# Two output chunks leave PSUM through ScalarE, and the first group's down products stand in another order

## The chip, the cores and the metric

The kernel runs on one core of a Trainium2 chip. The metric is device time in microseconds (us) of one execution. The engines of a core work side by side, each through its own queue of instructions in order, and wait for each other through semaphores: TensorE (PE, matrix products into PSUM banks), VectorE (DVE), ScalarE (ACT), GpSimd (POOL) and SyncE (SP, whose queue here issues most DMA transfers). PEld is TensorE's loading of weights, which runs beside its products.

## The reference

A gated linear recurrence per batch and head, then a layer with a softmax-weighted activation, a norm and a second product:

```python
for t in range(S):                       # S = 768, B = 4, H = 8, D = 48
    state = alpha[:, :, t, :, None] * state + k[:, :, t] (outer) v[:, :, t]
    y[:, :, t] = q[:, :, t] @ state
x = y.transpose(0, 2, 1, 3).reshape(B * S, H * D)        # 3072 x 384
h = x @ w_in                                             # 3072 x 1024
solu = h * softmax(h)
ln = (solu - mean(solu)) / sqrt(var(solu) + 1e-6) * g_ln
out = ln @ w_out                                         # 3072 x 384
```

All in float32 on the device; the weights come as float64 and are turned into float32 by bit operations.

## The kernel before

**Tiling.** The 768 tokens are cut into G = 6 groups of 128 per batch; one group holds 4 batches x 128 = 512 tokens. A *chunk* n = 4g + b is the 128 tokens of batch b in group g. For each group the kernel does the attention part, then the `up` product (eight blocks f of 128 columns of h, each 128 x 512), and the `down` product per chunk: eight steps f accumulate 128 x 385 in one PSUM bank (`down`, L491; column 385 is the sum of the row that the norm needs). `down(n, half)` does four steps; with `part` only some of them. In float32 each step is two TensorE instructions.

**Attention of a group a.** `alpha_T` (L202, VectorE) transposes alpha; `scan_back` (L221, three scans on VectorE) makes the products of the decays; `keys_T` and `keys` (L234, L238, VectorE and GpSimd) make the scaled keys; `scan_on` (L225, three scans, i = 2, 0, 1) makes the factors of the queries, and with i = 2 also the small ScalarE copy `fend` (L231). `decay` (L253, GpSimd) scales the running state; `scores` (L272, TensorE) writes four PSUM banks `a0` to `a3`; `masked` (L286, VectorE) moves them to SBUF under the causal mask; `read_state` and `read_values` (L327, L340, TensorE) make y in the same four banks, and ScalarE copies y to `x` (L348), which `up` reads. `next_state` (L350) adds the group's keys and values to the state.

**Activation.** `up_act` (L392): ScalarE takes the exp e of h from PSUM (L400), VectorE u = h e (L401), ScalarE u squared (L402). `running` sums e and u squared; `token_sums` (L444) turns those sums into one number per token.

**`finish(n)`** (L502): VectorE copies the row sum out of the bank, forms the variance (three small operations, L514 to L519), and, in group 0 only, adds the mean correction into an SBUF tile `o_mean` (L523, reading the bank); GpSimd takes the power -1/2 (L527), ScalarE scales into `o_sb` (L529), SP writes it out (L530). There are two `o` banks (`ps_o`, two buffers), so `down` of chunk n + 2 can start only when chunk n has left its bank. Tiles named `o_mean` and `o_sb` have two buffers each.

**Checks.** The fast path is valid only where alpha lies in range and the float64 weights do. `alpha_over(g)` (L207, ScalarE, two passes over 128 x 1536) counts alphas outside; the next `load(alpha, an, g + 1)` overwrites what it reads, so that load (four DMAs on SP) waits for it. `in_range(i)` (L569, ScalarE, four instructions) does the like for the weight piece i. Nothing but the end of the kernel waits for their counts.

**What sets the order.** It is written out by hand: `tc.manual_schedule()` keeps each engine's instructions in program order. Group 0 and the attention of groups 1 and 2 are straight code (L639 to L804). `mean(0)` and `mean(1)` (L615) make the mean of the weights' rows; `tq` are the transposed queries. From group 1 on, a loop over g and eight steps s reads from a table which pieces of attention of group g + 1 go where (`first` for g = 1, L814; `usual` for the later ones, L808): `head` comes ahead of the step's `up`, `behind` after it, `middle` and `tail` around the step's `down`.

Of the kernel before, what the change touches and what calls it, by code (L numbers as in the profile page):

```python
# [9 lines left out]
FP = mybir.dt.float32  # L10
# [6 lines left out]
P = 128  # L17
# [15 lines left out]
def fast_path(ctx, tc, q, k, v, alpha, moe_w_in, moe_w_out, moe_g_ln, out):  # L33
# [12 lines left out]
    nc = tc.nc  # L46
    B, H, S, D = q.shape
    NTOK, DM = out.shape
# [8 lines left out]
    HF = FC // 2  # L57
# [4 lines left out]
    def pool(name, bufs, **kw):  # L62
        return ctx.enter_context(tc.tile_pool(name=name, bufs=bufs, **kw))
# [4 lines left out]
    work = pool("work", 2)  # L68
# [31 lines left out]
    an = const.tile([P, H, TQ, D], FP, name="an")  # L100
# [33 lines left out]
    st = [dict() for _ in range(N)]  # L134
# [3 lines left out]
    def load(src, dst, g):  # L138
        t = slice(g * P, (g + 1) * P)
        for b in range(B):  # L140
            nc.sync.dma_start(
                out=dst[32 * b : 32 * b + 32].rearrange("t h u d -> t h (u d)"),
                in_=src[b, :, t, :].rearrange("h (t u) d -> t h (u d)", u=TQ),
            )
# [62 lines left out]
    def alpha_over(g):  # L207
        x = an.rearrange("p h u d -> p (h u d)")
        sq = one.tile([P, 768], FP, name="sq").bitcast(U8)[:, 0 : x.shape[1]]
        for i, sign in enumerate((1.0, -1.0)):  # L210
            nc.scalar.activation(  # L211
                out=sq, in_=x, func=AF.Relu, scale=sign, bias=mone, accum_out=over[:, g, i : i + 1]
            )
# [12 lines left out]
    def scan_on(g, i):  # L226
        part = slice(NP * i, NP * i + NP)
        if i == 2:

            nc.vector.reciprocal(out=seed[:, :, 0:1], in_=h4[:, :, 1:2])  # L230
            nc.scalar.copy(out=fend[:, g], in_=h4[:, :, 1])  # L231
        scan(aT[:, part], aT[:, part], seed[:, part], False)
# [33 lines left out]
    def quarter(b):  # L266
        return slice(32 * b, 32 * b + 32)
# [4 lines left out]
    def scores(g, half, a=None):  # L272
        a = a or banks("a", [NP, P])
        for i in range(NP):
            h = half * NP + i
            for kb, qb in ((h, h), (H + h // 2, H + h)):
                for b in range(B):
                    nc.tensor.matmul(  # L278
                        a[b][:, i], lhsT=kT[quarter(b), kb], rhs=qv[quarter(b), qb], start=kb == h, stop=kb != h,
                        tile_position=(32 * b, 0), skip_group_check=True,  # L280
                    )
        masks[half] = a
# [11 lines left out]
    def keys_back(g, t=None):  # L294
        t = t or banks("tp", [NP, P], 3)
        for j in range(NB):
            nc.tensor.transpose(out=t[j // NP][:, j % NP], in_=kT[:, j], identity=ident)  # L297
        for i in range(3):
            nc.scalar.copy(out=kg[:, NP * i : NP * i + NP], in_=t[i])
# [191 lines left out]
    def down(n, half, part=slice(0, HF)):  # L491
        g, b = divmod(n, B)
        d = st[n]
        if half == 0 and part.start == 0:
            d["o"] = ps_o.tile([P, 512], FP, tag="o", name="o")
        for f in range(half * HF + part.start, half * HF + part.stop):
            nc.tensor.matmul(  # L497
                d["o"][:, 0 : DM + 1], lhsT=u_of(g, f)[:, b * P : b * P + P], rhs=w_out[:, f], start=(f == 0),
                stop=(f == FC - 1), skip_group_check=True,
            )  # L500

    def finish(n):  # L502
        g, b = divmod(n, B)
        d = st[n]
        s, o = sums[:, n], d["o"][:, 0:DM]
        t0 = b * S + g * P
        if g == G - 1:
            o_sb = work.tile([P, DM], FP, name="o_sb")
            r = gr[g]["r"][:, b : b + 1]
            nc.scalar.activation(out=o_sb, in_=o, func=AF.Copy, scale=r)  # L510
            nc.scalar.dma_start(out=out[t0 : t0 + P, :], in_=o_sb)
            d.clear()
            return
        nc.vector.tensor_copy(out=s[:, 0:1], in_=d["o"][:, DM : DM + 1])  # L514
        t = small.tile([P, 1], FP, name="t")
        nc.vector.scalar_tensor_tensor(
            out=t, in0=s[:, 0:1], scalar=-1.0 / DFF, in1=s[:, 0:1], op0=ALU.mult, op1=ALU.mult
        )
        nc.vector.tensor_tensor(out=s[:, 3:4], in0=t, in1=gr[g]["s"][:, b : b + 1], op=ALU.add)  # L519
        if g == 0:  # L520

            o = work.tile([P, DM], FP, name="o_mean")
            nc.vector.scalar_tensor_tensor(  # L523
                out=o, in0=mean_sb, scalar=s[:, 0:1], in1=d["o"][:, 0:DM], op0=ALU.mult, op1=ALU.add
            )
        r = small.tile([P, 1], FP, name="r")
        nc.gpsimd.tensor_tensor(out=r, in0=s[:, 3:4], in1=mhalf, op=ALU.pow)  # L527
        o_sb = work.tile([P, DM], FP, name="o_sb")
        nc.scalar.activation(out=o_sb, in_=o, func=AF.Copy, scale=r)  # L529
        nc.sync.dma_start(out=out[t0 : t0 + P, :], in_=o_sb)  # L530
        d.clear()
# [35 lines left out]
    made = {}  # L567

    def in_range(i):  # L569


        if not float64:
            return
        hi = raws[i][:, :, :, 1].bitcast(FP)
        sq = one.tile([P, F], FP, name="sq").rearrange("p (c f) -> p c f", c=hi.shape[1])
        nc.scalar.activation(out=sq, in_=hi, func=AF.Square, accum_out=far[:, i, 0:1])  # L576
        nc.scalar.activation(out=sq, in_=sq, func=AF.Exp, scale=-(2.0**24), accum_out=far[:, i, 1:2])  # L577
# [37 lines left out]
    def mean(half):  # L615


        m = ps_h.tile([P, 512], FP, tag="h", name="sums")[:, 0:DM]
        if half == 0:
            for f in range(FC):  # L620
                r = quarter(f % 4)
                nc.tensor.matmul(
                    m[r], lhsT=ones[:, 0:32], rhs=w_out[:, f, 0:DM], start=f < 4, stop=f >= FC - 4,
                    tile_position=(0, r.start), skip_group_check=True,
                )
            made["m"] = work.tile([P, DM], FP, name="o_mean")
            nc.scalar.mul(out=made["m"], in_=m, mul=-1.0 / (32 * DFF))
        else:
            nc.tensor.matmul(m, lhsT=ones, rhs=made["m"], start=True, stop=True)
            nc.scalar.copy(out=mean_sb, in_=m)  # L630
# [32 lines left out]
    def three(name, where):  # L663
        return [pool.tile([P, NP, P], FP, tag=tag, name=f"{name}{i}") for i, (pool, tag) in enumerate(where)]
# [12 lines left out]
    for i in range(3):  # L677
        part = slice(NP * i, NP * i + NP)
# [6 lines left out]
    for i in (2, 0, 1):  # L685
        if i == 1:
            scan_on(0, i)
        part = slice(NP * i, NP * i + NP)
        nc.vector.tensor_tensor(  # L689
            out=qe if i == 2 else qv[:, part], in0=t[i], in1=aT[:, part, 1:SW], op=ALU.mult  # L690
# [62 lines left out]
    for i in range(3):  # L753
        scan_back(1, i)
        part = slice(NP * i, NP * i + NP)
        nc.vector.tensor_tensor(out=kT[:, part], in0=tk[i], in1=hk[:, part], op=ALU.mult)
    mean(0)
    down(0, 1)
    mean(1)
    in_range(5)  # L760
    in_range(6)
    down(1, 1)
    tq += three("tp_q2", [(ps_h, "h")])
    turned(qn, ends_q, tq, range(H, NB))
    load(q, qn, 2)
    keys_back(1, three("tp", [(ps_a, "a2"), (ps_a, "a3"), (ps_h, "h")]))
    scan_on(1, 2)
    nc.vector.tensor_tensor(out=qe, in0=tq[2], in1=aT[:, H:NB, 1:SW], op=ALU.mult)
    apart()
    finish(0)  # L770
    decay(1)
    in_range(7)
    for i in range(2):
        scan_on(1, i)
        part = slice(NP * i, NP * i + NP)
        nc.vector.tensor_tensor(out=qv[:, part], in0=tq[i], in1=aT[:, part, 1:SW], op=ALU.mult)
    down(2, 0)
    scores(1, 0)
    finish(1)
    alpha_over(1)  # L780
    load(alpha, an, 2)
    masked(0)
    down(2, 1)
    scores(1, 1)
    masked(1)
    finish(2)
    alpha_T(2)
    read_begin()
    for batches, part in (((0, 1), slice(0, HF // 2)), ((2, 3), slice(HF // 2, HF))):
        down(3, 0, part)  # L790
        for n in range(len(parts)):
            read_state(n, batches)
    alpha_over(2)
    load(alpha, an, 3)
    for i in range(3):
        scan_back(2, i)
    keys_T(2)
    keys(2)
    load(k, kn, 3)
    scan_on(2, 2)  # L800
    scan_on(2, 0)
    read_values(1)
    down(3, 1)
    finish(3)  # L804


# [3 lines left out]
        behind={0: "states v keys", 1: "load on2 on0 on1", 2: "lasts firsts", 3: "apart", 5: "decay", 6: "alpha", 7: "back"},  # L810
# [2 lines left out]
    )  # L813
    first = dict(  # L814
        head={3: "keys_back", 5: "masked0", 6: "masked1"},
        behind={0: "states v", 1: "on1", 2: "lasts firsts", 3: "apart", 5: "decay", 7: "alpha back"},
        tail={4: "scores0", 5: "scores1", 6: "begin read0 read1"},
        middle={7: "read2 read3 values"},
    )
# [51 lines left out]
    for g in range(1, G + 1):  # L871
# [10 lines left out]
        for s in range(FC):  # L882
# [17 lines left out]
            if step:  # L900
                n, half = step
# [23 lines left out]
    def compare(out, x, bound, op):  # L925
# [6 lines left out]
        out=chunks[:, :, 2], in0=sums[:, :, 2], scalar=0.25, in1=sums[:, :, 3], op0=ALU.mult, op1=ALU.is_le  # L932
# [6 lines left out]
    else:  # L939
# [9 lines left out]
        out=bad, in0=all_ok[0:1, 0:1], scalar1=float(P * ends[-1]), scalar2=None, op0=ALU.is_lt  # L949
# [451 lines left out]
```

## Time and profile before

| what | value |
|---|---|
| time, median of 4 runs (lowest to highest) | 383.97 us (383.59 to 384.51) |
| the profiled execution's own time | 383.94 us |
| its span | 382.1 us |
| TensorE busy | 367.4 us, 96% |
| VectorE busy | 245.3 us, 64% |
| ScalarE busy | 144.6 us, 38% |
| GpSimd busy | 125.6 us, 33% |
| mean granted clock of TensorE | 0.996 |

A line of the timeline reads: start in us, length in us, engine, source line, operation, output <- inputs, sizes, and xcount instructions taken together; in square brackets the time that the engine sat idle before it and what ended that idle time ("issue" means nothing that the profile shows). The lengths of matrix products are modelled and overlap the next one a little, so the time of a group is best read from its start to the start of the next. A line of the table of windows gives a stretch, its length, the busy time of each engine with its number of instructions, the clock granted to TensorE (1.00 is full speed), the busy share of the DMA engines and GB/s.

The stretch that the change touches lies between 66 and 145 us. Around it, in the profiled execution:

| what | start, us | length, us |
|---|---|---|
| `finish(0)` on VectorE | 80.80 | 0.97 |
| its power on GpSimd | 81.41 | 0.54 |
| `decay(1)` on GpSimd, six pieces | 81.91 | 4.54 |
| `finish(1)` on VectorE | 85.51 | 1.19 |
| alpha's check of group 1 on ScalarE | 87.70 | 3.35 |
| `masked(0)`, `masked(1)` on VectorE | 88.53, 93.32 | 2.48, 2.49 |
| load of alpha for group 2 issued by SP | 91.08 | 1.82 |
| alpha's check of group 2 on ScalarE | 97.44 | 3.35 |
| the four copies of y by ScalarE | 103.20 | 1.81 |
| first `up` product of group 1 | 107.13 | 2.74 |

### The profile page before, as it was taken

The numbers are of one execution on the slowest core, as the hardware profiler recorded it, in microseconds if no ns is written. First come the engines' busy times: TensorE is split into PE (matmuls) and PEld (weight loads), VectorE is DVE, ScalarE is ACT, GpSimd is POOL, SyncE is SP. The second block draws the span as 40 slices with busy tenths as digits, with TensorE's granted clock in tenths as the row PEclk, the third lists the DMA queues.
The fourth block names the chain that finished last, engine by engine and source line by source line (L and its number), as shares of the span: only waits on it lengthen the run. The fifth ranks groups of instructions, "written<-read, shape, count | busy, mean of one in ns | idle before, by whom it ended". The sixth has DMA issues, their size and how long they took to land.

```text
span 382.1 us, 10525 instructions
## 1 busy us (share of the span) xinstructions
PE 367.4 (96%) x4665; PEld 221.1 (58%) x4665; DVE 245.3 (64%) x381; ACT 144.6 (38%) x258; POOL 125.6 (33%) x132
## 2 busy tenths in 40 slices
PE   8789999879999999999999999999999999999995
PEld 8675355546755666555576555576555665555552
DVE  0999879995989866893565884665875411554410
ACT  2628774384525244124252224351224131233111
POOL 5020000041055990544621553630562520333210
PEclk9999999989999999999999999999999999999999
DMA  9992989304457100961000960001500000000011
GB/s 185 181 313 93 220 277 158 84 21 103 104 123 114 40 4 4 185 145 43 22 3 25 205 144 23 22 10 40 81 0 22 22 24 2 21 21 21 22 44 49
DMA packets 65510, 30.78 MB, mean 81 GB/s; under 512 B 47016, under 2 KB 63664, under 8 KB 65456
## 3 DMA queue, kind: packets, MB, share of 16 engines
q1 hardware_dynamic: 64432, 29.10, 34.7%
q10 hardware_dynamic: 1024, 0.92, 0.7%
q8 instruction: 38, 0.62, 0.7%
q14 instruction: 16, 0.13, 0.1%
HBM read 25.30 MB, written 4.72 MB: 79 GB/s over the span
## 4 chain that ended last, share of the span: by engine, by line
PE 75%; DVE 12%; ACT 5%; issue 3%; SPq 2%; DMA 2%; ACTq 0%; DVEq 0%
PE o L497 31%; PE h L386 25%; PE y L312 10%; PE a L278 5%; DVE room L401 2%; SPq L153 2%; DMA qn<-in_q_dram 2%; PE kv L361 1%; DVE sT L289 1%; ACT sq L576 1%; DVE top L592 1%; DVE hT L219 1%; ACT sq L577 1%; PE tp L297 1%; ACT sT L400 1%
## 5 line engine op out<-in xcount | busy, mean ns | idle before, releaser
L497 PE MATMUL o<-w_out,room 128*128 128x385 f32 x384 | 135.3, 496 | 2.4 <-DVE o_mean L523 2.4
L386 PE MATMUL h<-x,w_in 128*128 128x512 f32 x288 | 132.2, 598 | 0.2 <-DVE g_col L613 0.2
L497 PEld LDWEIGHTS o<-w_out,room 128*128 128x128 f32 x384 | 72.1, 192 | 59.3 <-issue 17.8
L386 PEld LDWEIGHTS h<-x,w_in 128*128 128x128 f32 x288 | 53.0, 189 | 58.9 <-issue 48.7
L401 DVE TENSOR_TENSOR room<-h,e 128x512 f32<-128x512 f32 x40 | 27.5, 689 | 82.3 <-ACT e L400 82.3
L400 ACT ACTIVATE e<-h 128x512 f32<-128x512 f32 x40 | 23.9, 597 | 108.3 <-PE h L386 108.3
L527 POOL TENSOR_TENSOR r<-sums,mhalf 128x1 f32<-128x1 f32 x20 | 14.3, 715 | 138.4 <-DVE sums L519 138.4
L417 POOL TENSOR_TENSOR p<-p,e 128x512 f32<-128x512 f32 x30 | 41.8, 1393 | 15.7 <-ACT e L400 15.6
L402 ACT ACTIVATE u<-room 128x512 f32<-128x512 f32 x40 | 25.2, 631 | 35.1 <-DVE room L401 35.1
L289 DVE TENSOR_TENSOR sT<-a,mask 128x512 f32<-128x512 f32 x44 | 27.3, 682 | 10.0 <-PE a L278 10.0
L219 DVE TENSOR_TENSOR_SCAN hT<-aT,unit 128x516 f32<-128x516 f32 x18 | 23.1, 1347 | 8.3 <-ACT aT L671 8.2
L240 POOL TENSOR_TENSOR kT<-kT,hT 128x1024 f32<-128x1024 f32 (+1 forms) x8 | 14.2, 1795 | 42.4 <-DVE kT L194 42.4
L219 DVE TENSOR_TENSOR_SCAN aT<-aT,seed 128x516 f32<-128x516 f32 x18 | 27.2, 1540 | 0.2
L417 DVE TENSOR_TENSOR p<-p,u 128x512 f32<-128x512 f32 x30 | 23.1, 769 | 6.5 <-ACT u L402 6.5
L278 PEld LDWEIGHTS a<-qv,kT 32*128 32x128 f32 x704 | 21.7, 186 | 8.1 <-issue 2.4
L312 PE MATMUL y<-sT,vn 128*32 128x128 f32 x768 | 23.7, 274 | 2.4 <-issue 1.4
L278 PE MATMUL a<-qv,kT 32*128 32x128 f32 x704 | 24.5, 278 | 1.3 <-DVE qv L689 0.8
L312 PEld LDWEIGHTS y<-sT,vn 128*32 128x32 f32 x768 | 21.0, 110 | 4.6 <-issue 3.2
L211 ACT ACTIVATE sq<-an,mone 128x1536 uint8<-128x1536 f32 x12 | 18.8, 1570 | 0.2
L312 PE MATMUL y<-qv,state 32*32 32x128 f32 x960 | 16.5, 277 | 0.0
L529 ACT ACTIVATE o_sb<-o,r 128x384 f32<-128x384 f32 x16 | 9.3, 581 | 18.7 <-POOL r L527 18.7
L312 PEld LDWEIGHTS y<-qv,state 32*32 32x32 f32 x960 | 12.1, 103 | 6.9 <-issue 4.9
(140 smaller groups left out, 365.4 us busy)
## 6 DMA issues: line engine op xcount, KB each, us to landing
an<-in_alpha_dram SPq DMA_DIRECT2D x20, 192.0 KB, 4.1
vn<-in_v_dram SPq DMA_DIRECT2D x10, 384.0 KB, 5.3
out_dram<-o_sb SPq DMA_DIRECT2D x20, 192.0 KB, 1.9
room<-in_moe_w_in_dram SPq DMA_DIRECT2D x6, 512.0 KB, 8.1
room<-in_moe_w_out_dram SPq DMA_DIRECT2D x8, 384.0 KB, 3.9
kn<-in_k_dram SPq DMA_DIRECT2D x16, 192.0 KB, 4.3
qn<-in_q_dram SPq DMA_DIRECT2D x16, 192.0 KB, 3.7
kn<-in_k_dram SPq DMA_DIRECT2D x4, 384.0 KB, 5.8
```

Source lines behind the costliest of these rows:

```text
L211: nc.scalar.activation(out=sq, in_=x, func=AF.Relu, scale=sign, bias=mone, accum_out=over[:, g, i : i + 1])
L219: nc.vector.tensor_tensor_scan(out=o, data0=a, data1=s, initial=1.0, op0=ALU.mult, op1=ALU.add)
L278: nc.tensor.matmul(a[b][:, i], lhsT=kT[quarter(b), kb], rhs=qv[quarter(b), qb], start=kb == h, stop=kb != h, tile_position=(32 * b, 0), sk ...
L289: nc.vector.tensor_tensor(out=sT[:, b, half * NP : half * NP + NP], in0=a[b], in1=mask[:, None, :].to_broadcast([P, NP, P]), op=ALU.mult,)
L312: nc.tensor.matmul(y_bank(b)[quarter(r), a], lhsT=lhsT, rhs=rhs, start=(b, r) not in begun, stop=stop, tile_position=(row, 32 * r), skip_g ...
L386: nc.tensor.matmul(h, lhsT=w_in[:, a, f * P : (f + 1) * P], rhs=d["x"][:, a].rearrange("p b t -> p (b t)"), start=(a == 0), stop=(a == KC ...
L400: nc.scalar.activation(out=e, in_=h, func=AF.Exp)
L401: nc.vector.tensor_tensor(out=u, in0=h, in1=e, op=ALU.mult)
L402: nc.scalar.activation(out=u2, in_=u, func=AF.Square)
L417: eng.tensor_tensor(out=p, in0=d[0][i] if f == 1 else p, in1=d[f][i], op=ALU.add)
L497: nc.tensor.matmul(d["o"][:, 0 : DM + 1], lhsT=u_of(g, f)[:, b * P : b * P + P], rhs=w_out[:, f], start=(f == 0), stop=(f == FC - 1), skip ...
L527: nc.gpsimd.tensor_tensor(out=r, in0=s[:, 3:4], in1=mhalf, op=ALU.pow)
```

## The change

Four things, all in the straight code and in the table `first`:

- A new helper `moved(n)` copies a finished chunk (128 x 385, row sum included) by ScalarE from its PSUM bank into an SBUF tile `o_mean`. It is called for chunks 0 and 1 right behind their last `down` step. `finish(0)` and `finish(1)` then read that tile instead of the bank and add the mean correction in place; they stand later, between `masked(0)` and `masked(1)`. The `o_mean` tiles become 385 columns wide.
- The `down` steps stand elsewhere: two steps of `down(0, 1)` ahead of `mean(0)` and two behind it; `down(2, 1)` directly behind `down(2, 0)`, ahead of `scores(1, 0)`; `down(3, 0)` ahead of `scores(1, 1)`; two steps of `down(3, 1)`, then one, between the reads of the state, and the last one behind `read_values(1)`.
- ScalarE's checks stand elsewhere: `in_range(6)` behind the copy of chunk 1, `alpha_over(1)` and the load of alpha behind it ahead of `finish(0)` and `finish(1)`, `alpha_over(2)` and its load behind the copies of y. On SP the load of alpha for group 2 so comes ahead of the outputs of chunks 0 and 1, and that for group 3 behind the load of k.
- `scan_on(2, 0)` moves out of the straight code into step 1 of group 1 ("on0 on1" where "on1" stood).

On GpSimd the power of chunk 0 now comes behind `decay(1)` instead of ahead of it.

```diff
+    def moved(n):
+
+        o = work.tile([P, DM + 1], FP, name="o_mean")
+        nc.scalar.copy(out=o, in_=st[n]["o"][:, 0 : DM + 1])
+        st[n].update(o=o, moved=True)
+
     def finish(n):
...
         if g == 0:
 
-            o = work.tile([P, DM], FP, name="o_mean")
+            if not d.get("moved"):
+                o = work.tile([P, DM + 1], FP, name="o_mean")[:, 0:DM]
             nc.vector.scalar_tensor_tensor(
                 out=o, in0=mean_sb, scalar=s[:, 0:1], in1=d["o"][:, 0:DM], op0=ALU.mult, op1=ALU.add
             )
...
-            made["m"] = work.tile([P, DM], FP, name="o_mean")
+            made["m"] = work.tile([P, DM + 1], FP, name="o_mean")[:, 0:DM]
...
+
+    down(0, 1, slice(0, 2))
     mean(0)
-    down(0, 1)
+    down(0, 1, slice(2, HF))
+    moved(0)
     mean(1)
     in_range(5)
-    in_range(6)
     down(1, 1)
+    moved(1)
     tq += three("tp_q2", [(ps_h, "h")])
     turned(qn, ends_q, tq, range(H, NB))
     load(q, qn, 2)
+    in_range(6)
     keys_back(1, three("tp", [(ps_a, "a2"), (ps_a, "a3"), (ps_h, "h")]))
     scan_on(1, 2)
     nc.vector.tensor_tensor(out=qe, in0=tq[2], in1=aT[:, H:NB, 1:SW], op=ALU.mult)
     apart()
-    finish(0)
     decay(1)
     in_range(7)
...
     down(2, 0)
+    down(2, 1)
     scores(1, 0)
-    finish(1)
     alpha_over(1)
     load(alpha, an, 2)
     masked(0)
-    down(2, 1)
+    finish(0)
+    finish(1)
+    down(3, 0)
     scores(1, 1)
     masked(1)
     finish(2)
     alpha_T(2)
     read_begin()
-    for batches, part in (((0, 1), slice(0, HF // 2)), ((2, 3), slice(HF // 2, HF))):
-        down(3, 0, part)
+    for batches, part in (((0, 1), slice(0, 2)), ((2, 3), slice(2, 3))):
+        down(3, 1, part)
         for n in range(len(parts)):
             read_state(n, batches)
-    alpha_over(2)
-    load(alpha, an, 3)
     for i in range(3):
         scan_back(2, i)
     keys_T(2)
     keys(2)
     load(k, kn, 3)
     scan_on(2, 2)
-    scan_on(2, 0)
     read_values(1)
-    down(3, 1)
+    alpha_over(2)
+    load(alpha, an, 3)
+    down(3, 1, slice(3, HF))
     finish(3)
...
-        behind={0: "states v", 1: "on1", 2: "lasts firsts", 3: "apart", 5: "decay", 7: "alpha back"},
+        behind={0: "states v", 1: "on0 on1", 2: "lasts firsts", 3: "apart", 5: "decay", 7: "alpha back"},
```

## The prediction

> **What bounds the kernel now.** I read the page's first part, then the chain that ended last, then TensorE's timeline and VectorE's in the stretch that the change touches, and last a table of windows for the clock.
>
> ```profile
> PE 367.4 (96%) x4665; PEld 221.1 (58%) x4665; DVE 245.3 (64%) x381; ACT 144.6 (38%) x258; POOL 125.6 (33%) x132
> PE 75%; DVE 12%; ACT 5%; issue 3%; SPq 2%; DMA 2%; ACTq 0%; DVEq 0%
> ```
>
> TensorE (PE) is busy 96% of the 382.1 us, and three quarters of the chain is its own. So only its holes can be won, and what lengthens no hole costs nothing. From about 145 us on TensorE runs without a hole worth naming: whatever is won before 145 us reaches the end unchanged. The holes in the stretch that the change touches:
>
> ```profile
> 69.49 1.63 PE L622 MATMUL sums<-w_out,ones 128*32 128x384 f32 x16 [0.98 <-DVE cols L457]
> 82.00 4.52 PE L497 MATMUL o<-w_out,room 128*128 128x385 f32 x8 [2.39 <-DVE o_mean L523]
> 102.49 2.02 PE L312 MATMUL y<-sT,vn 128*32 128x128 f32 x65 [0.76 <-issue]
> ```
>
> The number in brackets is the idle time before the group and what ended it. The middle one is the large one. `down(2, 0)` wants a PSUM bank, and both `o` banks belong to chunks 0 and 1 until VectorE has run `finish(0)`, which stands late in its queue. The group behind that hole is slow too: 4.52 us for eight instructions, where 74.39 to 77.07 gives 2.68 for the same eight. The windows say why; the number after the busy times is the granted clock:
>
> ```profile
> 80.00:82.00 2.00, 0.00 (x0) 0.03 (x1) 1.83 (x7) 1.64 (x4) 0.59 (x2) 1.00 0.00 0
> 82.00:84.00 2.00, 2.00 (x4) 1.26 (x5) 1.97 (x3) 1.97 (x5) 1.90 (x3) 0.60 0.16 61
> 84.00:86.00 2.00, 2.00 (x4) 0.98 (x4) 1.93 (x4) 0.61 (x2) 2.00 (x3) 0.54 0.10 38
> 86.00:88.00 2.00, 2.00 (x54) 1.55 (x56) 0.77 (x3) 0.82 (x2) 1.04 (x3) 1.00 0.00 0
> ```
>
> The hole costs 2.39 us and then 1.8 us of half clock. The last view is the chain where group 1 starts (VectorE and ScalarE):
>
> ```profile
> 106.06 4.48 DVE L219 TENSOR_TENSOR_SCAN aT<-aT,seed 128x516 f32<-128x516 f32 x2
> 111.64 0.61 ACT L529 ACTIVATE o_sb<-o_mean,r 128x384 f32<-128x384 f32 x1 [6.62 <-POOL r L527]
> 112.16 0.58 ACT L400 ACTIVATE e<-h 128x512 f32<-128x512 f32 x1
> 115.39 1.80 DVE L219 TENSOR_TENSOR_SCAN aT<-aT,seed 128x516 f32<-128x516 f32 x1
> 123.80 2.01 PE L278 MATMUL a<-qv,kT 32*128 32x128 f32 x56 [0.21 <-ACT qv L244]
> 130.09 1.86 PEld L278 LDWEIGHTS a<-qv,kT 32*128 32x128 f32 x58 [0.30 <-DVE sT L289]
> ```
>
> The first `h` of group 1 is ready at 109.8, but its exp waits for 112.16: `finish(3)`'s output stands before it in ScalarE's queue and waits on two scans, GpSimd's keys and its power. From there to 132 us VectorE and ScalarE set the pace (scores at 123.80 wait for `qv`, those at 130.09 for the masks).
>
> **Part 1: chunks 0 and 1 leave their banks by ScalarE; downs reordered.** Added: two copies 128x385 on ScalarE, 0.5 us each by the 128x384 copy L630 (0.48). They fall at about 72.8 and 76.1, where ScalarE sits idle (2.94 us before L630) or runs range checks that nobody waits for; with `in_range(6)` moved behind the second copy (76.6 to 78.6) the key copies L299 end near 80.1 (80.44 in before), ahead of every user. Now TensorE's queue, with lengths between starts in the profile. At 68.50 it is free; two steps of `down(0, 1)` (2.70/2 = 1.35) fill the 0.98 hole; mean's sixteen (1.56) end at 71.4, two more steps at 72.75, the second mean (0.64) at 73.4, `down(1, 1)` (2.68) at 76.1, the queries' last quarter (1.01) at 77.1, eight of the twelve key transposes at 78.1. The last four need VectorE's third `kT`, which stays at 68.11 + its unchanged queue = 78.68: a new hole of 0.6, ending at 79.25. Then `down(2, 0)` and `down(2, 1)` (2 x 2.70) run at once, since their bank came free at 73.3, and end at 84.65. In before, `scores(1, 0)` started at 86.45 with `down(2, 1)` still to do.
>
> `scores(1, 0)` also needs both `qv` parts and their banks from VectorE. Its queue loses `finish(0)` there (80.80 to 81.77: 0.97), so the second `qv` (85.51 in before) ends near 84.6: a tie with TensorE. GpSimd's `decay` stood behind `finish(0)`'s power at 81.41; now it starts at 76, beside other scans. In before the scans beside it kept 1.23 us, GpSimd's own pieces stretched (L261 1.25 and 0.44), and one small VectorE operation took 0.39 instead of 0.16. So the price lies between nothing and the three GpSimd pieces that a scan can meet (3 x 0.49 = 1.5); I take 0.25, by the 0.23 seen. `scores(1, 0)` then runs 84.9 to 86.9.
>
> **Part 2: `finish(0)` and `finish(1)` between the masks.** `masked(0)` takes 86.95 to 89.4 (2.48). Both finishes (0.97 each, and again 0.25) end at 91.6. TensorE meanwhile does `down(3, 0)` (2.70) to 89.6 and `scores(1, 1)` (2.0) to 91.6: again a tie, so the 2 us of VectorE are covered, and with a shorter cover they would show one for one. `masked(1)` runs 91.65 to 94.1, against 93.32 to 95.8: 1.7 earlier. `finish(2)`, `alpha_T(2)` and the three scans keep their lengths and end at 101.15 instead of 102.85. `alpha_T(2)` needs its load: alpha's check now starts at 84.2 on ScalarE (after `in_range(7)`) and SP issues the load near 87.6 instead of 91.08, ahead of the outputs, so with 1.8 to issue and about 4 to land it is there by 93.5.
>
> The Trainium skill, SBUF — State Buffer, on what VectorE and GpSimd share, says that a VectorE instruction with two SBUF inputs and a GpSimd one that reads SBUF exclude each other for their whole length, the first to start winning. It speaks against this change, because `o_mean` now comes from SBUF where `o` came from PSUM, so the mean's addition has two SBUF inputs beside GpSimd's power, and because `decay` moves among scans. By it alone each of the two powers (0.54) could be added once, 1.1 in all, and the sum below would be 1.4 instead of 2.5. No row of before shows exactly this pair.
>
> **Part 3: start of group 1.** TensorE: two steps of `down(3, 1)` to 92.95, reads 1.78, one step 0.67, reads 1.77 to 97.2, values 3.98 to 101.15 (to 101.9 if the 0.76 "issue" hole stands), the last step to 102 or 102.6. ScalarE: `fend` waits for the scans (101.3), then four copies of y (1.81) to 103.1. So `h` starts at 103.15 instead of 107.13: 4.0 earlier, after a hole of 0.5 to 1.2, because one down step is left where four covered the copies. alpha's check of group 2 (3.35) moves behind those copies: 103.1 to 106.5. It delays nothing if the output of `finish(3)` is not ready before 106.5. That follows from VectorE: keys_T (2.86) to 104.0, reciprocal 0.35, one scan 2.24 to 106.6, `finish(3)`'s operand 0.52 later. GpSimd's keys start 1.7 earlier, at 103.5, and take 3.32 (as at 155.98) to 4.24 (beside two scans); I take 3.7, since one scan is left beside them, so they end at 107.2. Power 0.54 and output 0.6 put the exp at 108.4: 3.75 earlier, and the check is hidden by some 1.2 us. load(k, 3) keeps its place behind the key transposes (1.7 earlier); alpha's load for group 3 comes after it near 106.6, and v and q follow at 110 and later, before 112.74 and 121.38, used only from 139 us on.
>
> **Part 4: the scan that moved.** `scan_on(2, 0)` now stands in step 1 of group 1, ahead of `p`, `room` and the transposes that feed GpSimd's queries and the scores: on the path that sets the pace there. Its price is between 1.20 (a scan alone, at 159 to 163) and 2.24 (each of the two at 106.06). I take 1.25, because of the two scans only the first lies beside GpSimd's `p`, as the one in before (1.80) did already. TensorE, 4.0 early, waits for it before the scores.
>
> **The sum.** 3.75 - 1.25 = 2.5 us earlier at the scores of group 2, from 132 us on all TensorE's. The profiled execution took 383.94 (span 382.1 and 1.84 around it), 0.03 under the median of 383.97. So 381.5.
>
> **The clock.** Holes of 1.43 (before 14.96), 1.03 and 0.98 left the clock at 1.00; the one of 2.39 halved it for about 3.4 us. The new holes (0.6, 1.2, and before the scores near 119 to 121 one of about 1.3 and one of 0.6) are each below. The last two together come to 1.9 and are undecided. One closing costs up to 4.52 - 2.70 = 1.8.
>
> The Trainium skill, TensorE: Matmul & The Clock Gate, section "Why this matters for your kernels", puts the limit at idle gaps above about 3 us. By it the hole of 2.39 should have cost no clock, which this trace contradicts; by its limit none of the new holes costs anything and the sum stays 2.5, by the row a lumped hole makes it 0.7.
>
> **Rivals.** (a) Forecast, 380.6 to 382.4. (b) The gate closes once in the new hole before the scores near 120 us: 2.5 - 1.8, 383.3. For it: the two waits lie close. Against: each is below 1.43. (c) The moved scan is absorbed in VectorE's waits for ScalarE (0.70 before several `p`): up to 4.0 is kept, 380.0. Against: the row after the scan has no idle time before it. (d) The gain is swallowed: the first exp moves, but VectorE (13.86 of 16 us busy from 107 to 123) with both scans contended at 2.24 and queries behind them gives all back: 383.9. Against: that needs 3.75, and the scan is 2.24 at most. (e) Slower, by the shared access of VectorE and GpSimd: `decay`, whose six pieces were 4.54 us of GpSimd at 81.91 to 86.6, moves among the scans that `scores(1, 0)` waits for. If GpSimd wins every meeting, VectorE loses up to 4.5 there, which is on the path since that point is a tie; above 2.5 the change is slower, at worst by 2.0, 386.0. For it: the contended scans at 106.06. Against: in before the scans beside the same pieces kept 1.23.
>
> **How the numbers follow.** Chances: (a) 0.62, (b) 0.12, (c) 0.08, (d) 0.08, (e) 0.10. About 0.2% (0.8 us) is what a measurement of this kernel can tell from no change. (b) lies at that bound and counts half to each side: faster 0.62 + 0.08 + 0.06 = 0.76, same 0.08 + 0.06 = 0.14, slower 0.10. The range goes from (c), 380.0, to above (b), 383.5, leaving out (d) and (e).
>
> **What the profile after would show.** No hole before `down(2, 0)` and no half clock at 82 to 86; `scores(1, 0)` near 85; first `h` of group 1 near 103 and its exp near 108.4; two scans before `p` in step 1, the first about 1.8; the scores of group 2 ending near 123.2 instead of 125.7. The forecast is wrong if the clock falls below 1.00 anywhere between 100 and 125, if scans at 76 to 84 take more than 1.4, or if the exp waits for alpha's check.

## The result

The changed kernel took 382.48 us (median of 46 executions, 381.51 to 387.18) against 384.48 us for the kernel before (72 executions beside it, 383.18 to 388.97). The ratio is 0.9952, with a 95% interval of 0.9936 to 0.9968: faster by 1.8 us, between 1.2 and 2.5. The forecast was 2.5 us, the upper end of that interval. It put the time at 381.5 us, from the 383.97 us of the four executions that it had of the kernel before; beside the changed kernel that one took 384.48 us. The profiled execution took 381.55 us (span 379.8), against 383.94 (span 382.1) before.

Executions of one kernel scatter by several microseconds: in four of the profiled ones (scan_in_place, check_in_place, copies_early_load, after again) the clock is halved once near 27 us, long before the change. Positions are therefore given from the start of the queries' turn (`tp_q` out of `qn` on TensorE). It lies at 68.5 to 70.0 us in those four, at 66.55 us before and at 66.18 us after: 0.37 of the 2.39 us between the two spans was there before the first changed instruction. What follows the first `down` step of group 1 (`down(4, 0)`) lasted 237.1 us in both profiles, so the rest, 2.0 us, lies in the stretch that the change touches.

The page of the changed kernel (busy time of each engine, then the chain that ended last):

```profile
PE 366.7 (97%) x4665; PEld 220.5 (58%) x4665; DVE 245.2 (65%) x381; ACT 145.4 (38%) x260; POOL 126.6 (33%) x132
PE 72%; DVE 17%; ACT 4%; issue 2%; SPq 2%; DMA 2%; POOL 0%; DVEq 0%; ACTq 0%
```

TensorE has the same 4665 products and is still what bounds the kernel; ScalarE has the two copies more. TensorE's timeline after:

```profile
78.39 0.66 PE L297 MATMUL tp<-ident,kT 128*128 128x128 f32 x4 [0.58 <-DVE kT L763]
78.89 5.35 PE L497 MATMUL o<-w_out,room 128*128 128x385 f32 x16
84.17 2.24 PE L278 MATMUL a<-qv,kT 32*128 32x128 f32 x64
...
102.75 2.83 PE L386 MATMUL h<-x,w_in 128*128 128x512 f32 x6
...
120.62 0.50 PE L278 MATMUL a<-qv,kT 32*128 32x128 f32 x8 [1.26 <-POOL qv L251]
121.45 2.01 PE L278 MATMUL a<-qv,kT 32*128 32x128 f32 x56 [0.33 <-ACT qv L244]
```

The hole of 2.39 us ahead of `down(2, 0)` is gone. In its place stands one of 0.58, ahead of the last key transposes, and the sixteen `down` instructions behind it take 5.35, full speed. The table of windows after shows the clock there (the number behind the five engines): 1.00 where before had 0.60 and 0.54.

```profile
82.00:84.00 2.00, 2.00 (x7) 0.95 (x5) 1.97 (x3) 1.94 (x5) 0.00 (x0) 1.00 0.00 0
84.00:86.00 2.00, 2.00 (x59) 1.83 (x61) 0.29 (x1) 1.97 (x3) 0.00 (x0) 1.00 0.04 8
```

Then the other engines' timelines after, from the finishes to the start of group 1:

```profile
90.09 0.61 DVE L530 SCALAR_TENSOR_TENSOR o_mean<-mean_sb,sums,o_mean 128x384 f32<-128x384 f32 x1
91.21 2.48 DVE L289 TENSOR_TENSOR sT<-a,mask 128x512 f32<-128x512 f32 x4 [0.51 <-PE a L278]
...
94.59 2.06 DVE L194 STREAM_TRANSPOSE aT<-an 128x1024 f32<-128x1024 f32 x1
...
106.41 0.91 DVE L522 SCALAR_TENSOR_TENSOR t<-sums 128x1 f32<-128x1 f32 x1
...
111.79 2.95 DVE L219 TENSOR_TENSOR_SCAN aT<-aT,seed 128x516 f32<-128x516 f32 x2
...
108.17 0.61 ACT L536 ACTIVATE o_sb<-o_mean,r 128x384 f32<-128x384 f32 x1 [2.23 <-POOL r L534]
108.69 0.58 ACT L400 ACTIVATE e<-h 128x512 f32<-128x512 f32 x1
...
89.28 1.84 POOL L534 TENSOR_TENSOR r<-sums,mhalf 128x1 f32<-128x1 f32 x2 [7.33 <-DVE sums L525]
...
103.06 4.25 POOL L240 TENSOR_TENSOR kT<-kT,hT 128x1024 f32<-128x1024 f32 x2 [8.21 <-PE o L497]
107.59 0.55 POOL L534 TENSOR_TENSOR r<-sums,mhalf 128x1 f32<-128x1 f32 x1 [0.29 <-DVE sums L525]
```

VectorE is done with both finishes before the scores are (idle 0.51 ahead of `masked(1)`), it finds alpha already loaded (no idle time ahead of the transposition at 94.59), and the exp of group 1 still waits for the output of `finish(3)`, as before, but at 108.69 instead of 112.16. The two scans in step 1 take 2.95 where the one before took 1.80.

Gains at each point, the 0.37 taken off:

| point | before, us | after, us | gain |
|---|---|---|---|
| `scores(1, 0)` | 86.45 | 84.17 | 1.9 |
| `masked(1)` on VectorE | 93.32 | 91.21 | 1.7 |
| the last steps of `down(3, 1)`, behind the values | 104.43 | 102.00 | 2.1 |
| first `h` of group 1 | 107.13 | 102.75 | 4.0 |
| its exp | 112.16 | 108.69 | 3.1 |
| scores of group 2 (the 56) | 123.80 | 121.45 | 2.0 |
| `down(4, 0)` | 145.03 | 142.63 | 2.0 |

The step from 2.1 to 4.0 is the order of the downs: before, four steps stood between the values and the first `h` (2.70 from start to start), after, one (0.75); the other three now run where TensorE had waited. TensorE's timeline at the last point, in before and then in after:

```profile
145.03 2.86 PE L497 MATMUL o<-w_out,room 128*128 128x385 f32 x8
...
142.63 2.86 PE L497 MATMUL o<-w_out,room 128*128 128x385 f32 x8
```

### The profile page after: what moved, and what is told of

Read it like the earlier page. It is cut to its first block, busy times and chain, and to the rows that moved or that the text cites. A ratio compares the mean times of both kernels' runs of the same rounds, so it can differ in the third digit from the quotient of the medians.

```text
span 379.8 us, 10525 instructions
## 1 busy us (share of the span) xinstructions
PE 366.7 (97%) x4665; PEld 220.5 (58%) x4665; DVE 245.2 (65%) x381; ACT 145.4 (38%) x260; POOL 126.6 (33%) x132
## 4 chain that ended last, share of the span: by engine, by line
PE 72%; DVE 17%; ACT 4%; issue 2%; SPq 2%; DMA 2%; POOL 0%; DVEq 0%; ACTq 0%
PE o L497 30%; PE h L386 25%; PE y L312 7%; PE a L278 5%; DVE sT L289 2%; DVE room L401 2%; SPq L153 2%; DVE hT L219 2%; DMA qn<-in_q_dram 2%; PE kv L361 1%; DVE top L599 1%; DVE aT L194 1%; DVE aT L219 1%; DVE low L607 1%; DVE top L596 1%
## 5 line engine op out<-in xcount | busy, mean ns | idle before, releaser
L497 PE MATMUL o<-w_out,room 128*128 128x385 f32 x384 | 133.8, 491 | 0.0
L497 PEld LDWEIGHTS o<-w_out,room 128*128 128x128 f32 x384 | 71.2, 190 | 55.8 <-issue 13.7
L260 POOL TENSOR_TENSOR state<-state,hT 128x192 f32<-128x192 f32 x20 | 11.3, 581 | 55.9 <-DVE hT L219 55.9
L219 DVE TENSOR_TENSOR_SCAN aT<-aT,seed 128x516 f32<-128x516 f32 x18 | 26.3, 1491 | 0.2
```

What stands on the lines that cost most here:

```text
L219: nc.vector.tensor_tensor_scan(out=o, data0=a, data1=s, initial=1.0, op0=ALU.mult, op1=ALU.add)
L497: nc.tensor.matmul(d["o"][:, 0 : DM + 1], lhsT=u_of(g, f)[:, b * P : b * P + P], rhs=w_out[:, f], start=(f == 0), stop=(f == FC - 1), skip ...
```

## The experiments

My theory: the gain is made ahead of `scores(1, 0)`, handed on by VectorE's queue to the start of group 1, and cut there to what `finish(3)`'s output allows, less the price of the moved scan. The rivals: the gain is only the half clock that is gone; it comes from the reordered downs or from the moved scan; the places of alpha's checks add or cost something of their own. All positions count from the queries' turn; ratios stand against the kernel before on the same chip (95% interval in brackets).

| kernel | `h` | scores of group 2 | `down(4, 0)` | ratio |
|---|---|---|---|---|
| before | 40.58 | 57.25 | 78.48 | |
| after | 36.57 | 55.27 | 76.45 | 0.9952 [0.9936, 0.9968] |
| after, again | 36.62 | 55.20 | 76.64 | 0.9955 [0.9925, 0.9986] |
| scan_in_place | 36.97 | 55.39 | 76.87 | 0.9979 [0.9951, 1.0007] |
| check_in_place | 36.97 | 55.24 | 77.43 | 0.9939 [0.9903, 0.9976] |
| copies_only | 40.38 | 57.47 | 78.59 | 1.0013 [0.9980, 1.0046] |
| warm_in_hole | 40.28 | 57.12 | 77.81 | 1.0010 [0.9982, 1.0038] |
| copies_early_load | 41.00 | 57.97 | 79.32 | 1.0015 [0.9984, 1.0046] |
| copies_load_warm | 39.76 | 56.43 | 77.11 | 0.9997 [0.9967, 1.0026] |
| check1_late | 44.05 | 64.25 | 85.72 | 1.0162 [1.0111, 1.0213] |
| finish3_late | 36.93 | 54.79 | 76.01 | 0.9910 [0.9878, 0.9942] |
| after_fill | 36.61 | 55.31 | 76.00 | 0.9938 [0.9913, 0.9964] |
| best | 36.57 | 53.37 | 75.01 | 0.9891 [0.9848, 0.9934] |

### copies_only: the kernel before with the two copies alone

```diff
     down(0, 1)
+    moved(0)
     mean(1)
...
     down(1, 1)
+    moved(1)
```

The helper `moved` and `finish` as in the change; both finishes, all downs, checks and scans stand where they stood.

> The kernel before with the two ScalarE copies alone: chunks 0 and 1 leave their banks by ScalarE, everything else stands where it stood. Theory (the hole of 2.39 us and the half clock go, but the scores behind `down(2, 0)` then wait for VectorE's second `qv`, which still has `finish(0)` ahead of it): `scores(1, 0)` starts near 85.6 instead of 86.45, the clock stays at 1.00, and the whole is 0.8 us faster than before. Rival (the freed bank is the whole of the gain, orders are nothing): 2.0 us faster than before.

The hole ahead of `down(2, 0)` and the half clock are gone, and the kernel is no faster: 1.0013, and 0.1 us later at `down(4, 0)`. Timelines of TensorE and VectorE in copies_only:

```profile
83.64 0.48 PE L278 MATMUL a<-qv,kT 32*128 32x128 f32 x2 [1.55 <-DVE qv L785]
85.51 2.06 PE L278 MATMUL a<-qv,kT 32*128 32x128 f32 x62 [1.38 <-DVE sums L520]
...
96.91 2.09 DVE L194 STREAM_TRANSPOSE aT<-an 128x1024 f32<-128x1024 f32 x1 [1.09 <-DMA an<-in_alpha_dram]
```

TensorE now waits ahead of `scores(1, 0)` instead: 1.55 for the first `qv` part of L785, which still stands behind `finish(0)` and a scan, and 1.38 more, until 85.51. The profile puts these down to `finish(1)`'s first reading (L520, 85.37 to 85.51); but the second `qv` part, one scan later in VectorE's queue, ended just before it, at 85.45, and the scores need that part. The 0.8 us that are left (62 of the scores at 19.08 from the turn, against 19.90) are lost at the next wait, on a DMA: VectorE reaches the transposition of alpha early and waits 1.09 for a load that before had arrived unnoticed. The copies, and the hole and the half clock that go with them, bring by themselves nothing that these runs can tell; the interval leaves room for 0.8 us.

### warm_in_hole: the hole filled with idle products

```diff
+    warm(5, ps_h, "h")
     down(2, 0)
     scores(1, 0)
```

The kernel before, with five products of ones that nobody reads (ten TensorE instructions) in front of `down(2, 0)`: the wait stays, the clock is kept.

> The kernel before with five idle matrix products (ones by ones, 128 wide, some 1.6 us on TensorE) put into the hole ahead of `down(2, 0)`, in a bank that is free from 80.9 on; `down(2, 0)` still waits for its bank until 82.0. Theory (the gate closes because the hole is long, and it costs 1.8 us of which all but 0.8 us is covered by VectorE's second `qv`): the clock stays at 1.00, `down(2, 0)` takes 2.7 us instead of 4.5, and the whole is 0.7 us faster than before. Rival A (the half clock has another cause than the hole): the clock still falls to 0.5 at 82, no gain. Rival B (the half clock is wholly on the path): 1.8 us faster.

The clock stayed at 1.00, and `scores(1, 0)` stood 0.8 us earlier (full group at 19.11), again followed by a wait of VectorE for alpha:

```profile
96.39 2.07 DVE L194 STREAM_TRANSPOSE aT<-an 128x1024 f32<-128x1024 f32 x1 [0.73 <-DMA an<-in_alpha_dram]
```

At `down(4, 0)` 0.7 was gained in the profile; the times show nothing (1.0010). The interval, 0.9982 to 1.0038, lies wholly above that of the change, so the half clock alone does not explain the result.

### copies_early_load and copies_load_warm: the load of alpha earlier

The first is copies_only with alpha's check and load ahead of `finish(1)`, the second has thirteen idle products (26 instructions) besides:

```diff
     down(2, 0)
+    warm(13, ps_h, "h")          # in copies_load_warm alone
     scores(1, 0)
-    finish(1)
     alpha_over(1)
     load(alpha, an, 2)
+    finish(1)
```

> The kernel with the two copies alone, and alpha's check of group 1 with the load behind it moved ahead of `finish(1)` (some 3.1 us earlier on ScalarE). Theory (what the copies gained, 0.8 us at the scores, was lost to a new wait, 1.1 us of VectorE for alpha's load ahead of its transposition): that wait is gone, the transposition starts near 95.8 instead of 96.9, and the whole is 0.9 us faster than with the copies alone and than before. Rival (the loss was the holes without releaser in the reads of the state, which were 0.4 us longer with the copies alone): the transposition starts earlier but the whole stays within 0.3 us of the copies alone.

The wait for the load was gone, but in this profile the clock closed in the wait ahead of `scores(1, 0)`, and those took 3.69 instead of 2.06. TensorE's timeline in copies_early_load:

```profile
86.38 0.48 PE L278 MATMUL a<-qv,kT 32*128 32x128 f32 x2 [1.57 <-DVE qv L785]
88.25 3.69 PE L278 MATMUL a<-qv,kT 32*128 32x128 f32 x62 [1.39 <-DVE sums L520]
```

The same two waits had left the clock alone in copies_only. That asked for the second kernel:

> The kernel with the two copies and the earlier load of alpha, and thirteen idle matrix products (3.1 us) filling TensorE's wait between `down(2, 0)` and `scores(1, 0)`. Theory (that wait, 1.6 and 1.4 us with a short group between, half closed the clock and hid what copies and load had won): the clock stays at 1.00 there, `scores(1, 0)` takes 2.0 us instead of 3.7, and the whole is 0.9 us faster than before. Rival (bank and load together win nothing): the clock stays, and the whole is within 0.2 us of before.

With that wait filled the clock stayed at 1.00 throughout and `down(4, 0)` came 1.4 us earlier than in before. The times do not confirm it (0.9997, from 0.9967 to 1.0026): behind `down(4, 0)` this execution took 1.1 us longer, of which a hole of 0.74 just before 199.75, among the reads of the state and values, is one piece. What copies and an earlier load are worth together without the reordered downs stays open between nothing and about 1.3 us. So does the share of the reordered downs and the later finishes: no run has them without copies and load. Against this kernel's profile the change is 0.7 earlier at `down(4, 0)`; by the times (0.9997 and 0.9952) nearly all of the gain could be theirs.

### check1_late: the load of alpha late again

```diff
-    alpha_over(1)
-    load(alpha, an, 2)
     masked(0)
     finish(0)
     finish(1)
+    alpha_over(1)
+    load(alpha, an, 2)
     down(3, 0)
```

The changed kernel, with alpha's first check behind the two outputs in ScalarE's queue and its load behind them in SP's.

> The changed kernel with alpha's check of group 1 and the load behind it put back behind `finish(0)` and `finish(1)` alone. Theory (the load has to be early, or the wait for it takes the place of the one removed): on ScalarE the check then runs from 91.8 to 95.1 behind the two outputs, the load lands near 101, VectorE's transposition starts there instead of at 94.6, and the whole is 6 us slower than the changed kernel, 4 us slower than before. Rival (the load has slack, the gain is the bank and the order of the downs): within 0.5 us of the changed kernel.

It cost 9.3 us at `down(4, 0)` against the change, more than the 6 that I had expected; by the times this kernel is 6.2 us slower than the kernel before (1.0162). VectorE waits 7.50 for the load, TensorE then 5.74 for `x`, and the clock closes for two windows on top of it. Timelines and windows of check1_late:

```profile
102.61 2.09 DVE L194 STREAM_TRANSPOSE aT<-an 128x1024 f32<-128x1024 f32 x1 [7.50 <-DMA an<-in_alpha_dram]
...
110.68 5.15 PE L386 MATMUL h<-x,w_in 128*128 128x512 f32 x6 [5.74 <-ACT x L348]
```

```profile
108.50:111.90 3.40, 1.22 (x2) 0.70 (x3) 3.37 (x5) 3.00 (x6) 0.98 (x1) 0.51 0.00 0
111.90:115.30 3.40, 3.40 (x6) 1.14 (x4) 3.33 (x5) 1.96 (x4) 3.26 (x2) 0.50 0.74 168
```

The moved check and load, which look like housekeeping, are thus a part without which the rest of the change would be a loss: a check that nobody waits for holds back a load that VectorE waits for.

### scan_in_place: the moved scan put back

```diff
     scan_on(2, 2)
+    scan_on(2, 0)
     read_values(1)
...
-        behind={0: "states v", 1: "on0 on1", 2: "lasts firsts", ...},
+        behind={0: "states v", 1: "on1", 2: "lasts firsts", ...},
```

> The changed kernel with `scan_on(2, 0)` back in its old place, ahead of `finish(3)`. Theory (the scan is paid wherever it stands, less in front of the exp's chain than it saves there): two scans of about 2.3 us each stand before `finish(3)`, so the first exp of group 1 comes 1.5 us later than the 108.7 of the changed kernel; step 1 then has one scan and gives 1.1 us back, so the scores of group 2 are 0.4 us later and the whole is 0.3 to 0.5 us slower than the changed kernel, about 1.6 us faster than before. Rival A (in step 1 the scan lies in idle time of VectorE and is free): the whole is 1.5 us slower than the changed kernel. Rival B (the scan in step 1 costs all that it saved): no difference.

Against after, `down(4, 0)` came 0.42 us later. Timelines of VectorE and ScalarE in scan_in_place (its turn begins at 68.52):

```profile
106.28 4.47 DVE L219 TENSOR_TENSOR_SCAN aT<-aT,seed 128x516 f32<-128x516 f32 x2
...
115.46 1.83 DVE L219 TENSOR_TENSOR_SCAN aT<-aT,seed 128x516 f32<-128x516 f32 x1
...
112.38 0.58 ACT L400 ACTIVATE e<-h 128x512 f32<-128x512 f32 x1
```

Beside GpSimd's keys the two scans take 4.47; with one there (2.40 after) the first exp comes 1.35 earlier. In step 1, the pair takes 2.95 instead of 1.83, so 1.12 of that is paid back. The rows so leave 0.23 for the move; the positions give 0.12 at the scores of group 2 and 0.42 at `down(4, 0)`. So in the profiles most of the change's gain does not come from the move. The times alone cannot tell: 0.9979 against 0.9952 would be 1.0 us, and the two intervals overlap.

### check_in_place: alpha's second check put back

```diff
+    alpha_over(2)
+    load(alpha, an, 3)
     for i in range(3):
         scan_back(2, i)
...
     read_values(1)
-    alpha_over(2)
-    load(alpha, an, 3)
```

> The changed kernel with alpha's check of group 2 and the load behind it back in their old place, ahead of `scan_back(2)`. Theory (ScalarE is idle for 5.5 us before `fend` in the changed kernel, and the check in its new place ends 2.2 us before the output of `finish(3)` is ready, so both places are free): no difference to the changed kernel beyond 0.3 us. Rival (moving the check earned part of the gain, because `fend` and the copies of y stand behind it, or because the load on SP meets instruction fetches in `read_values`): 0.5 to 1.5 us slower than the changed kernel, with `fend` later than 101.0 or a longer gap without releaser in `read_values`.

Median 382.49 against the change's 382.48, ratios 0.9939 and 0.9952: its place behind the copies of y neither costs nor brings anything that these runs can tell. Up to the scores of group 2 the profile agrees with after (55.24 and 55.27). There the clock closed, in this execution. Windows and TensorE's timeline of check_in_place:

```profile
126.40:129.80 3.40, 3.40 (x35) 2.14 (x28) 2.71 (x4) 0.63 (x1) 3.32 (x3) 0.50 0.34 75
```

```profile
124.42 0.50 PE L278 MATMUL a<-qv,kT 32*128 32x128 f32 x8 [1.12 <-POOL qv L251]
125.25 2.72 PE L278 MATMUL a<-qv,kT 32*128 32x128 f32 x56 [0.32 <-ACT qv L244]
```

The two waits here (1.12 and 0.32) are shorter than those of after (1.26 and 0.33), where the clock stayed open. It cost 1.0 us at `down(4, 0)`.

### after, again, and after_fill: the wait before the scores of group 2 filled

The changed kernel was run once more as it is, and once with five idle products (ten instructions) ahead of those scores:

```diff
         elif what[:6] == "scores":
+            if a == 2 and what == "scores0":
+                warm(5)
             scores(a, int(what[6]))
```

> The changed kernel once more, on the chip of the runs beside it, to compare them directly. Theory: 2.0 us faster than before; VectorE's first long transposition for group 2 starts without waiting for the load of alpha; the wait ahead of the scores of group 2 is 1.6 us in two pieces.

> The changed kernel with five idle matrix products (1.2 us) in TensorE's wait ahead of the scores of group 2. Theory (the wait costs nothing by itself, it is VectorE's and GpSimd's; only where its two pieces fall into one clock window does it halve the clock): the scores start as in the changed kernel, within 0.15 us, the clock stays at 1.00 there, and the median is the same or up to 0.4 us faster than the changed kernel. Rival (the fill delays the scores): 0.3 to 1.0 us slower.

The change repeated itself: 0.9955, positions within 0.2 us. The filled wait left the scores where they were (55.31) and gave 0.9938: the same within the intervals. A closing at this place is therefore no large part of the usual time.

### finish3_late and best: the exp freed

The gain of 4.0 at `h` shrinks to 3.1 at the exp because `finish(3)`'s output stands ahead of it in ScalarE's queue. finish3_late puts `finish(3)` behind the first `up` of group 1, through the loop's own way of finishing a chunk; best besides moves the scan to step 0, into the idle time that this leaves on VectorE.

```diff
     down(3, 1, slice(3, HF))
-    finish(3)
...
-        after = None
+        after = 3 if g == 1 else None
...
-        behind={0: "states v", 1: "on0 on1", ...},
+        behind={0: "states v on0", 1: "on1", ...},      # in best alone
```

> The changed kernel with `finish(3)` moved behind the first up step of group 1, so that neither VectorE nor ScalarE has it ahead of the first exp. Theory (that exp waited for `finish(3)`, whose small operation stood 0.9 us behind GpSimd's keys): the exp starts near 106.2 instead of 108.7; the second exp is then bound by its own product (109.7), so 0.8 us is left at the scores of group 2 and the whole is 0.8 us faster than the changed kernel, 2.8 us faster than before. Rival A (VectorE pays for `finish(3)` a little later, so that nothing is won): within 0.2 us of the changed kernel. Rival B (the exp was all of it): 2.4 us faster than the changed kernel.

ScalarE and VectorE in finish3_late (turn at 66.95):

```profile
106.91 0.58 ACT L400 ACTIVATE e<-h 128x512 f32<-128x512 f32 x1
...
110.92 0.60 ACT L400 ACTIVATE e<-h 128x512 f32<-128x512 f32 x1 [0.97 <-PE h L386]
...
111.55 0.69 DVE L401 TENSOR_TENSOR room<-h,e 128x512 f32<-128x512 f32 x1 [1.30 <-ACT e L400]
```

The first exp comes 2.55 earlier than in after, at 39.96 from the turn against 42.51, but the second now waits for its product, and VectorE stands idle for 1.30 before it: only 0.5 reaches the scores and 0.4 `down(4, 0)`. So the exp's wait was real, and 2.1 of the 2.55 sit behind the next bound. The times of its six executions (0.9910) would be 1.6 us below the change, with intervals that overlap.

> The changed kernel with `finish(3)` behind the first up step and the moved scan one step earlier, behind the state's additions of step 0, where VectorE stood idle for 1.30 us before the second `room`. Theory (the scan was paid only because it stood ahead of `p` and `room` in step 1): the scan takes 1.2 to 1.3 us there beside no GpSimd work and delays nothing; the scores of group 2 come 1.2 us earlier than with `finish(3)` moved alone, and the whole is 1.6 us faster than the changed kernel, 3.6 us faster than before. Rival (the exp of step 1 or the product h is the bound there, so the scan is only moved into the same chain): no difference to `finish(3)` moved alone.

VectorE and TensorE in best (turn at 66.66):

```profile
109.60 1.22 DVE L219 TENSOR_TENSOR_SCAN aT<-aT,seed 128x516 f32<-128x516 f32 x1
110.99 0.69 DVE L401 TENSOR_TENSOR room<-h,e 128x512 f32<-128x512 f32 x1 [0.17 <-ACT e L400]
...
119.29 0.50 PE L278 MATMUL a<-qv,kT 32*128 32x128 f32 x8
120.03 2.01 PE L278 MATMUL a<-qv,kT 32*128 32x128 f32 x56 [0.24 <-ACT qv L244]
```

The scan runs in the idle time, which shrinks from 1.30 to 0.17, the wait of 1.26 before the scores is gone, and they come 1.9 earlier than in after. The time is 380.55 us (median of 6), 0.9891 of the kernel before with an interval of 0.9848 to 0.9934: 1.9 us below the change by the medians, and the lowest median of all kernels here; the interval overlaps that of finish3_late.

## Why the prediction was right, and where it was off

The time, 382.48, lies within the range of 380.0 to 383.5 and 0.1 above what (a) allowed. Of the 1.0 us between it and 381.5, 0.5 is the kernel before, which took 384.48 and not 383.97; the other 0.5 is the term of Part 3 below.

**Part 1 was right.** The copies cost nothing, the new hole was 0.58 (forecast 0.6), the half clock went, and `scores(1, 0)` came 1.9 us earlier where 1.6 had been forecast. The 0.25 allowed for `decay` beside the scans was not paid: the scans there took 1.22 to 1.26, so the slower rival (e), by the shared access, had nothing to work with.

**Part 2 was right.** The finishes cost VectorE 1.96 and lay under TensorE's work; `masked(1)` was 1.7 earlier, as forecast, and alpha's load was there. The rule of the Trainium skill, SBUF — State Buffer, section "Who interferes with whom", on what VectorE and GpSimd share was weighed as 1.1 us against the change. Its exclusion can be recognised: GpSimd's two powers took 0.87 and 0.86 (1.84 with the gap between them) where before each had taken 0.54 to 0.57, while VectorE's L530 kept its 0.61. But it was GpSimd that lost, and what was late were two outputs that nobody waited for. What the prediction passed over in one sentence, the earlier load, turned out in copies_only and check1_late to be the condition for the whole.

**Part 3 was right at `h` and short at the exp.** `h` came 4.0 earlier, as forecast, and alpha's second check was hidden, with 2.23 us of idle time behind it. The hole of 0.5 to 1.2 right before `h` did not appear: 0.52 of idle time that the profile puts down to nothing lay among the values instead. The exp came 3.1 earlier instead of 3.75. That is the mis-sized term. GpSimd's keys took 4.25, not the 3.7 that I had chosen between 3.32 and 4.24 because only one scan was left beside them; and the small L522 of `finish(3)`, priced at 0.16, took 0.91, until the keys ended, so that the power began 0.29 after them. The lone scan beside the keys took 2.40 against a forecast of 2.24. The row of two scans beside the keys (4.24 for the keys) was the right one for a single scan as well.

**Part 4 was right.** The pair of scans takes 1.15 more than the single one; the forecast was 1.25. So 3.1 - 1.15 = 2.0 instead of 2.5. Rivals (c) and (d) are out: the scan was neither absorbed nor was all the gain swallowed.

**The clock was right in its result and wrong in its reading.** No half clock stood between 100 and 125 us in the profile after. But that each hole stays below 1.43 is no safeguard: in check_in_place two of 1.12 and 0.32 closed it, which is rival (b), at 1.0 us instead of 1.8. That the clock stayed open in the profile after, with 1.26 and 0.33, seems in part luck. It depends on the execution, and the median holds some mixture that was not separated.

## What to carry to other kernels

A wait that is removed is worth only what the next queue can pass on: follow the gain to the loads and to the checks that hold a load's buffer, since the one here would have turned the same change into a loss of 6 us against the kernel before. A small instruction on VectorE beside a long GpSimd one can cost what is left of that one: L522 took 0.91 instead of 0.16, though the copy L520 beside the same keys kept 0.13. And where an idle gap opens behind the new bound, put the work there that you had to move, as best did.

## What the runs showed of the hardware that I had not expected

The granted clock changes on a grid. In every profile each stretch at full or half clock, from the first full one to the one before the last, lasted a whole multiple of 3.413 us: the half clock 3.413 (before, scan_in_place, check_in_place, copies_early_load, after again) or 6.827 (check1_late), the full clock, among others, 20.48 (6 times 3.413), 58.03 (17 times), 95.57 (28 times) or 296.96 (87 times). Where the grid lies differs from one execution to the next: the first full clock began at 3.90 us in before, 4.65 in after and 6.89 in check_in_place.

So whether one hole closes the clock seems partly chance, because it may be cut by a border of the grid. In copies_only the waits of 1.55 and 1.38 lay on either side of a border at 83.9 and the clock stayed; in after those of 1.26 and 0.33 had one at 120.7 between them; in copies_early_load almost all of the same two (2.8 us idle) fell between 85.0 and 88.4 and the clock closed. Before had 2.39 in one such stretch and closed. Idle time in a stretch is not the whole rule: check_in_place closed with 1.44 idle, between products of 32 rows, and check1_late did not with 1.9 between 98.3 and 101.7. What else counts is open. The Trainium skill, TensorE: Matmul & The Clock Gate, section "Why this matters for your kernels", names idle gaps above about 3 us; the closings at 2.39 and below disagree with it.

Among the reads of the state and values TensorE has short holes that wait for nothing that the profile shows, 0.18 to 0.80 us each and at other places from one execution to the next (2.17 in check1_late). They make two profiles of nearly the same kernel differ by some 0.5 us, so smaller differences of position, as in scan_in_place, settle nothing by themselves.
